# Two more Strassen-like pairs in a two-layer MLP behind attention, with their token sums made earlier and partly on another engine

## The chip, the cores and the metric

The kernel runs on one core of a Trainium2 chip. The metric is device time in microseconds (us), the median of three runs. A core has five engines with queues of their own that run in order: TensorE (PE) multiplies matrices into PSUM, VectorE (DVE) and ScalarE (ACT) compute on SBUF and PSUM, GpSimd (POOL) computes on SBUF, and SyncE (SP) issues the DMAs here. Semaphores order work between them.

## The reference, cut to what matters

```
attn = clustered attention over q, k, v            # batch 2, 8 heads, 768 tokens, 64 per head
x = attn as (1536 tokens, 512)
h = x @ w_in;  x = max(0.01 h, h) @ w_out          # layer one, d_ff 2048
h = x @ w_in2; r = max(h, 0); out = (r * r) @ w_out2   # layer two, d_ff 2048
```

All inputs are fp32 and the weights arrive as 64-bit floats that the kernel decodes itself.

## The kernel before

Each fp32 operand of a matmul is held as a rounded high part and the rest, the low part (xh and xl, wh and wl, gh and gl, th and tl), and each product is three matmuls: high by high, high by low, low by high. All of these matmuls are 128 x 128 by 512 columns.

After attention come two layers, m = 0 (layer one) and m = 1 (layer two). The 1536 tokens are three blocks b of 512 columns. The 2048 hidden rows are 16 slices f of 128, and the outer loop takes them in pairs (f, f + 1). For a pair, `g1` multiplies a block of x with a slice of w_in (12 matmuls, "a unit"), `act` turns the result into gh and gl, and `g2` multiplies these with a slice of w_out into four PSUM banks o0 to o3 (12 matmuls). After the second slice of a pair, `flush` adds the four banks to the running sum `acc` in SBUF; in a layer's first pair it copies them there on ScalarE (L860). In layer one's last pair `flush` makes the input of layer two: the sum (VectorE, L867), its high part xh (ScalarE, L868), and its low part xl (GpSimd, L869).

A pair is either plain or a quad. A plain pair runs six units. A quad (`quad`) computes blocks 0 and 1 of both slices together as a 2 by 2 problem with seven half products of 6 matmuls in place of eight (a Strassen-Winograd scheme); block 2 stays plain. It needs four differences of x, called t1 to t4 in the code: t1 = b12 - b11, t2 = b22 - t1, t3 = b22 - b12, t4 = b21 - t2, where b11 and b12 are a row chunk kk of x (0 or 1) in token blocks 0 and 1, and b21 and b22 the chunk 2 + kk. So each layer makes eight of them, once. th and tl hold t1 to t3; t4 takes the place of a part of x (`t_last`, L978 and L979). A quad also needs a third set of weights for each pair, sums of the two decoded slices (`sum_pieces`, four GpSimd operations at L197, a ScalarE cast, a GpSimd low part at L134).

PLAIN gives the number of plain pairs at the start of each layer. `step_list` gives the steps of a pair in TensorE's order; each engine gets its instructions in the order in which the steps are written out, except in layer one's first pair, which is ordered by a planner together with the end of attention. Steps of a plain pair are 12 matmuls each: units with the `g2` of earlier units between them. After step i of a pair, the table TURN issues pieces of the decoding of the next pair's weights: pieces 0 to 6 are the load (L147), a scaling on ScalarE (L156), three VectorE operations (L160, L166, L173), the high part on ScalarE (L133), and the low part on GpSimd (L134). The staging buffer `wraw` is single, so the load of a block waits for the last VectorE operation (L173) of the block before.

SUMS says after which step ("turn", counted from the start of the layer) the differences are made. In the kernel before, x is put together again from xh and xl on VectorE (`whole`, L960), the differences and low parts are made on GpSimd (L947 and L953), and the high parts on ScalarE (L950); the first of them come at turns 11 and 22 in layer one and 3 and 11 in layer two.

In layer two `act` is four instructions: relu (ScalarE, L803), square (VectorE, L806), high (ScalarE, L815) and low (VectorE, L818).

Of the kernel before, what the change touches and what calls it, by code (L numbers as in the profile page):

```python
# [8 lines left out]
F32 = mybir.dt.float32  # L9
# [4 lines left out]
ALU = mybir.AluOpType  # L14
# [39 lines left out]
def attention_moe_moe_kernel(  # L54
# [9 lines left out]
    nc = tc.nc  # L64
# [12 lines left out]
    NBLK = NT // N  # L77
    PLAIN = (3, 2)
    EARLY = 1
# [749 lines left out]
    def g2(m, b, f):  # L829
# [3 lines left out]
        for o in range(4):  # L833
# [20 lines left out]
            if last:  # L854
                flush(m, b, f // 2, o, outs[o])

    def flush(m, b, g, o, ps):
        a = acc[:, b, o]
        if g == 0:
            nc.scalar.copy(out=a, in_=ps)  # L860
            return
        if g < NF // 2 - 1:
            nc.vector.tensor_tensor(out=a, in0=ps, in1=a, op=ALU.add)  # L863
            return
        if m == 0:
            c = slice(b * N, (b + 1) * N)
            nc.vector.tensor_tensor(out=a, in0=ps, in1=a, op=ALU.add)  # L867
            nc.scalar.copy(out=xh[:, o, c], in_=a)  # L868
            nc.gpsimd.tensor_tensor(  # L869
                out=xl[:, o, c], in0=a, in1=xh[:, o, c].bitcast(F32), op=ALU.subtract  # L870
            )
        else:
            ob = tmp()
            nc.vector.tensor_tensor(out=ob, in0=ps, in1=a, op=ALU.add)
            r = b * N + o * 128
            nc.sync.dma_start(out=out[r : r + 128, :], in_=ob)
# [57 lines left out]

    def whole(k, b):
        h, l = x_in(k, b)
        t = tmp()
        nc.vector.tensor_tensor(out=t, in0=h.bitcast(F32), in1=l.bitcast(F32), op=ALU.add)
        return t

    def t_pieces(kk):

        st = {}

        def minus(out, x, y, *tag):
            st[out] = tmp(*tag)
            nc.gpsimd.tensor_tensor(out=st[out], in0=st[x], in1=st[y], op=ALU.subtract)  # L947

# [7 lines left out]

        def whole(out, k, b):
            h, l = x_in(k, b)
            st[out] = tmp()
            nc.vector.tensor_tensor(  # L960
                out=st[out], in0=h.bitcast(F32), in1=l.bitcast(F32), op=ALU.add
            )

        return [
            lambda: (whole("b12", kk, 1), whole("b11", kk, 0)),
            lambda: (minus("t1", "b12", "b11"), whole("b22", 2 + kk, 1)),
            lambda: (minus("t2", "b22", "t1"), high(0, "t1")),
            lambda: (low(0, "t1"), high(1, "t2")),
            lambda: (minus("t3", "b22", "b12"), whole("b21", 2 + kk, 0)),
            lambda: (low(1, "t2"), high(2, "t3")),  # L970
            lambda: (minus("t4", "b21", "t2", "t4", 2), t_late.update({kk: st["t4"]})),
            lambda: low(2, "t3"),
        ]

# [39 lines left out]
    )  # L1014
    SUMS = ((11, 22), (3, 11))
    LAST = (30, 19)
    order = ctx.enter_context(ExitStack())
# [10 lines left out]
    def pair_after(m, f):  # L1028
        return (m, f + 2) if f + 2 < NF else (m + 1, 0)

    prev = []
    for m in range(2):
        turn = 0
        sums = {}
        for kk in range(2):
            for i, t in enumerate(t_pieces(kk)):
                sums.setdefault(SUMS[m][kk] + i, []).append(t)
            sums.setdefault(LAST[m] + kk, []).append(lambda kk=kk: t_last(kk))
        for f in range(0, NF, 2):
# [14 lines left out]
            for i, step in enumerate(seq):  # L1054
                step()
                if (m, f, i) == (0, 0, 0):
                    for j in range(7):
                        piece((0, 0, 1), j)
                    piece((0, 2, 0), 0)
                for k, j in TURN[i] if i < len(TURN) else ():  # L1060
                    piece((*later, 0) if k == 3 else (*after, k), j)
                for t in sums.pop(turn, ()):
                    t()
                turn += 1
# [47 lines left out]
```

## Time and profile before

| what | value |
|---|---|
| median of 3 runs | 762.04 us (761.23 to 762.39) |
| the profiled execution | 762.55 us, of it span 760.8 us |
| granted TensorE clock | 1.0 of full speed |
| instructions in the span | 11079 |

The time of an execution is that of the whole program; the span is from the first instruction to the last one that the profiler saw. All times below are us from the start of the span. A matmul of 512 columns is shown as 0.39 us busy, but the next one starts 0.23 us after it; the ends overlap.

### The profile page before, as it was taken

What the parts mean: (1) busy time and instruction counts of PE and PEld (TensorE: products, weight loads), DVE (VectorE), ACT (ScalarE), POOL (GpSimd) and SP (SyncE); (2) the same over time, 40 slices, a digit from 0 to 9 for tenths busy, and PEclk for the clock granted to TensorE, in tenths of its full rate; (3) what the DMA queues carried; (4) which work ended last, traced back from release to release, by engine and by line L of the source; (5) the groups of instructions that cost most, each with busy time, mean ns of one, the idle gap of its engine ahead of it and who ended that gap; (6) DMA issues with size and microseconds to landing.
All of it is one profiled execution on the core that took longest, in us unless ns stands there. A gap on an engine that the chain in (4) does not pass through costs nothing.

```text
span 760.8 us, 11079 instructions
## 1 busy us (share of the span) xinstructions
PE 746.1 (98%) x4060; PEld 650.0 (85%) x4060; DVE 569.7 (75%) x861; ACT 440.4 (58%) x812; POOL 383.4 (50%) x344
## 2 busy tenths in 40 slices
PE   8999999999999999999999999999999999999998
PEld 8899999999989888888888888887878888888886
DVE  5999999999999545876666576656678787686755
ACT  6988988988998564344444343546544345443430
POOL 2889889889855326561442314356461441423400
PEclk9999999999999999999999999999999999999999
DMA  7494563572601212111121112203111211122004
GB/s 230 96 219 110 123 167 107 123 170 69 154 23 61 107 56 111 55 56 56 59 108 56 55 56 84 83 1 111 56 56 61 94 68 55 56 77 90 1 1 165
DMA packets 16902, 66.35 MB, mean 87 GB/s; under 512 B 3152, under 2 KB 4048, under 8 KB 11856
## 3 DMA queue, kind: packets, MB, share of 16 engines
q1 hardware_dynamic: 16848, 65.65, 29.1%
q8 instruction: 32, 0.52, 0.3%
q14 instruction: 22, 0.18, 0.1%
HBM read 44.60 MB, written 3.15 MB: 63 GB/s over the span
## 4 chain that ended last, share of the span: by engine, by line
PE 78%; DVE 13%; ACT 5%; issue 1%; DMA 1%; POOL 1%; DVEq 0%; SPq 0%; ACTq 0%; POOLq 0%
PE o L847 32%; PE h L770 29%; PE A L487 6%; PE S L389 5%; PE T L452 5%; DVE el L469 4%; DVE nm L412 3%; ACT e L422 2%; DMA wraw<-w 1%; PE warm L242 1%; DVE xt L509 1%; DVE ds L319 1%; ACT acc L860 1%; DVE m L318 1%; DVE h L806 1%
## 5 line engine op out<-in xcount | busy, mean ns | idle before, releaser
L134 POOL TENSOR_TENSOR wl<-wt,wh 128x1024 fp32r<-128x1024 f32 x32 | 77.0, 2407 | 132.8 <-ACT wh L133 132.8
L818 DVE TENSOR_TENSOR gl<-h,gh 128x512 fp32r<-128x512 f32 x96 | 65.8, 690 | 70.8 <-ACT h L813 50.2
L770 PE MATMUL h<-xl,wh 128*128 128x512 f32 x296 | 115.4, 390 | 0.0
L770 PE MATMUL h<-xh,wl 128*128 128x512 f32 x296 | 115.0, 389 | 0.0
L770 PE MATMUL h<-xh,wh 128*128 128x512 f32 x296 | 114.8, 390 | 0.0
L863 DVE TENSOR_TENSOR acc<-o,acc 128x512 f32<-128x512 f32 x144 | 92.6, 685 | 12.1 <-PE o L847 12.1
L469 DVE TENSOR_TENSOR el<-T,eh 128x512 fp32r<-128x512 f32 x144 | 94.4, 683 | 4.3 <-ACT eh L463 3.2
L439 POOL TENSOR_SCALAR e<-e,r 128x768 f32<-128x768 f32 x96 | 87.7, 925 | 19.4 <-DVE r L436 13.2
L412 DVE TENSOR_REDUCE nm<-S 128x1 f32<-128x768 f32 x96 | 90.9, 948 | 4.2 <-PE S L297 2.4
L422 ACT ACTIVATE e<-S,nm 128x768 f32<-128x768 f32 x96 | 87.3, 909 | 11.0 <-DVE nm L412 6.8
L389 PE MATMUL S<-hb 128*128 128x384 f32 (+1 forms) x384 | 90.2, 349 | 1.9 <-ACT e L422 1.2
L463 ACT CAST eh<-T 128x512 fp32r<-128x512 f32 x144 | 79.8, 589 | 13.4 <-PE T L452 13.1
L487 PE MATMUL A<-eh,vv 128*128 128x256 f32 x288 | 79.6, 306 | 2.0 <-DVE xt L509 2.0
L452 PE MATMUL T<-ident,e 128*128 128x128 f32 x576 | 79.6, 273 | 1.0 <-DVE el L469 1.0
L847 PE MATMUL o<-wh,gh 128*128 128x512 f32 x192 | 75.0, 391 | 2.8 <-DVE acc L863 1.7
L847 PE MATMUL o<-gl,wh 128*128 128x512 f32 x192 | 74.8, 390 | 0.0
L847 PE MATMUL o<-wh,gl 128*128 128x512 f32 x192 | 74.7, 389 | 0.0
L847 PE MATMUL o<-gh,wl 128*128 128x512 f32 x192 | 74.7, 389 | 0.0
L847 PE MATMUL o<-wl,gh 128*128 128x512 f32 x192 | 74.7, 389 | 0.0
L847 PE MATMUL o<-gh,wh 128*128 128x512 f32 x192 | 73.6, 389 | 0.0
L487 PE MATMUL A<-el,vv 128*128 128x256 f32 x288 | 72.5, 282 | 0.4 <-DVE el L469 0.4
L452 PEld LDWEIGHTS T<-ident,e 128*128 128x128 f32 x576 | 69.0, 144 | 4.0 <-POOL e L439 1.3
(130 smaller groups left out, 1537.1 us busy)
## 6 DMA issues: line engine op xcount, KB each, us to landing
wraw<-w SPq DMA_DIRECT2D x32, 1024.0 KB, 4.7
hb<-spl SPq DMA_DIRECT2D x14, 576.0 KB, 4.7
hb<-spl SPq DMA_DIRECT2D x42, 192.0 KB, 5.1
rqk<-qk SPq DMA_DIRECT2D x16, 384.0 KB, 3.8
rv<-v SPq DMA_DIRECT2D x8, 384.0 KB, 3.6
out<-q SPq DMA_DIRECT2D x12, 256.0 KB, 2.0
twice<-qk SPq DMA_DIRECT2D x8, 192.0 KB, 6.3
hb<-st SPq DMA_DIRECT2D x56, 24.0 KB, 2.0
```

The source lines that it names most:

```text
L134: return lambda: nc.gpsimd.tensor_tensor(out=wl, in0=t, in1=wh.bitcast(F32), op=ALU.subtract)
L389: nc.tensor.matmul(out=s[:, c, 0:HALF], lhsT=hb[0:k, a, i * 128 : (i + 1) * 128], rhs=hb[0:k, b, c * HALF : (c + 1) * HALF], start=(a == 0 ...
L412: nc.vector.tensor_reduce(out=n, in_=s_t[t][:, :, 0:HALF], axis=AX.XY, op=ALU.max, negate=True)
L422: nc.scalar.activation(out=e.rearrange("p (a b) -> p a b", a=2), in_=s_t.pop(t)[:, :, 0:HALF], func=AF.Exp, bias=n_t.pop(t), scale=1.0, ac ...
L439: nc.gpsimd.tensor_scalar(out=e_t[t], in0=e_t[t], scalar1=r_t[t // 2][:, t % 2 : t % 2 + 1], scalar2=1.0, op0=ALU.mult, op1=ALU.mult,)
L452: nc.tensor.transpose(T[:, o : o + 128], e_t[2 * u + b][:, kc * 128 : (kc + 1) * 128], ident)
L463: nc.scalar.copy(out=eh[:, 2 * g : 2 * g + 2, :].rearrange("p a b -> p (a b)"), in_=T_t[u, g])
L469: nc.vector.tensor_tensor(out=el[:, 2 * g : 2 * g + 2, :].rearrange("p a b -> p (a b)"), in0=T_t.pop((u, g)), in1=eh[:, 2 * g : 2 * g + 2, ...
L487: nc.tensor.matmul(out=A, lhsT=w, rhs=m[:, kc, :], start=(kc == 0 and i == 0), stop=(kc == KC - 1 and i == 1),)
L770: nc.tensor.matmul(out=out, lhsT=l, rhs=r, start=(first and i == 0), stop=(i == n - 1), skip_group_check=not first,)
L847: nc.tensor.matmul(out=outs[o], lhsT=l, rhs=r, start=(first and i == 0), stop=(last and i == 2),)
L863: nc.vector.tensor_tensor(out=a, in0=ps, in1=a, op=ALU.add)
```

## The change

Layer one has two plain pairs where it had three, and layer two one where it had two, so that one more pair in each layer is a quad. The differences of x are therefore made earlier: in layer one from turn 3 on, and in layer two from the last three steps of layer one (turns -3 to -1) to turn 3, with t4 put in place at turns 7 and 8. t1, t2 and t4 move from GpSimd to VectorE, t3 stays on GpSimd. Layer two takes x for them from `acc`, where layer one's fp32 outputs of blocks 0 and 1 stand, and no longer adds xh and xl up. For block 2, layer one's last sum is left in its PSUM bank, and its four low parts are made on VectorE, from PSUM, after the fourth sum; before, GpSimd made them from `acc`. In layer two's first pair the decode pieces 1 to 3 of the second weight block come a step later (TURN_SEAM).

```diff
--- before.py
+++ after.py
@@ -75,7 +75,7 @@
     HALF = S // 2
     N = 512
     NBLK = NT // N
-    PLAIN = (3, 2)
+    PLAIN = (2, 1)
     EARLY = 1
     RING = 6
     SIDE = 4
@@ -854,6 +854,8 @@
             if last:
                 flush(m, b, f // 2, o, outs[o])
 
+    x_low = []
+
     def flush(m, b, g, o, ps):
         a = acc[:, b, o]
         if g == 0:
@@ -864,11 +866,21 @@
             return
         if m == 0:
             c = slice(b * N, (b + 1) * N)
-            nc.vector.tensor_tensor(out=a, in0=ps, in1=a, op=ALU.add)
-            nc.scalar.copy(out=xh[:, o, c], in_=a)
-            nc.gpsimd.tensor_tensor(
-                out=xl[:, o, c], in0=a, in1=xh[:, o, c].bitcast(F32), op=ALU.subtract
-            )
+            x, eng = (ps, nc.vector) if b == 2 else (a, nc.gpsimd)
+            nc.vector.tensor_tensor(out=x, in0=ps, in1=a, op=ALU.add)
+            nc.scalar.copy(out=xh[:, o, c], in_=x)
+            if b == 2:
+                x_low.append((o, c, x))
+                if o < 3:
+                    return
+                todo = list(x_low)
+                x_low.clear()
+            else:
+                todo = [(o, c, x)]
+            for o, c, x in todo:
+                eng.tensor_tensor(
+                    out=xl[:, o, c], in0=x, in1=xh[:, o, c].bitcast(F32), op=ALU.subtract
+                )
         else:
             ob = tmp()
             nc.vector.tensor_tensor(out=ob, in0=ps, in1=a, op=ALU.add)
@@ -932,45 +944,61 @@
 
         return first, second, third
 
-    def whole(k, b):
-        h, l = x_in(k, b)
-        t = tmp()
-        nc.vector.tensor_tensor(out=t, in0=h.bitcast(F32), in1=l.bitcast(F32), op=ALU.add)
-        return t
-
-    def t_pieces(kk):
+    def t_ops(m, kk):
 
         st = {}
 
-        def minus(out, x, y, *tag):
-            st[out] = tmp(*tag)
-            nc.gpsimd.tensor_tensor(out=st[out], in0=st[x], in1=st[y], op=ALU.subtract)
-
-        def high(i, t):
-            nc.scalar.copy(out=th[:, i, kk], in_=st[t])
-
-        def low(i, t):
-            nc.gpsimd.tensor_tensor(
-                out=tl[:, i, kk], in0=st[t], in1=th[:, i, kk].bitcast(F32), op=ALU.subtract
-            )
-
         def whole(out, k, b):
+            if m:
+                st[out] = acc[:, b, k]
+                return
             h, l = x_in(k, b)
             st[out] = tmp()
             nc.vector.tensor_tensor(
                 out=st[out], in0=h.bitcast(F32), in1=l.bitcast(F32), op=ALU.add
             )
 
-        return [
-            lambda: (whole("b12", kk, 1), whole("b11", kk, 0)),
-            lambda: (minus("t1", "b12", "b11"), whole("b22", 2 + kk, 1)),
-            lambda: (minus("t2", "b22", "t1"), high(0, "t1")),
-            lambda: (low(0, "t1"), high(1, "t2")),
-            lambda: (minus("t3", "b22", "b12"), whole("b21", 2 + kk, 0)),
-            lambda: (low(1, "t2"), high(2, "t3")),
-            lambda: (minus("t4", "b21", "t2", "t4", 2), t_late.update({kk: st["t4"]})),
-            lambda: low(2, "t3"),
-        ]
+        def minus(eng, out, x, y, *tag):
+            st[out] = tmp(*tag)
+            eng.tensor_tensor(out=st[out], in0=st[x], in1=st[y], op=ALU.subtract)
+
+        def high(i, t):
+            nc.scalar.copy(out=th[:, i, kk], in_=st[t])
+
+        def low(i, t):
+            nc.gpsimd.tensor_tensor(
+                out=tl[:, i, kk], in0=st[t], in1=th[:, i, kk].bitcast(F32), op=ALU.subtract
+            )
+
+        def t4():
+            minus(nc.vector, "t4", "b21", "t2", "t4", 2)
+            t_late[kk] = st["t4"]
+
+        def t1():
+            if m:
+                whole("b12", kk, 1)
+                whole("b11", kk, 0)
+                whole("b22", 2 + kk, 1)
+                whole("b21", 2 + kk, 0)
+            minus(nc.vector, "t1", "b12", "b11")
+
+        return {
+            "w12": lambda: whole("b12", kk, 1),
+            "w11": lambda: whole("b11", kk, 0),
+            "w22": lambda: whole("b22", 2 + kk, 1),
+            "w21": lambda: whole("b21", 2 + kk, 0),
+            "t1": t1,
+            "t2": lambda: minus(nc.vector, "t2", "b22", "t1"),
+            "t3": lambda: minus(nc.gpsimd, "t3", "b22", "b12"),
+            "t4": t4,
+            "h1": lambda: high(0, "t1"),
+            "h2": lambda: high(1, "t2"),
+            "h3": lambda: high(2, "t3"),
+            "l1": lambda: low(0, "t1"),
+            "l2": lambda: low(1, "t2"),
+            "l3": lambda: low(2, "t3"),
+            "h4": lambda: t_last(kk),
+        }
 
     def t_last(kk):
         h, l = x_in(kk, 1)
@@ -1012,8 +1040,23 @@
         ((0, 1),), ((0, 2), (0, 3)), ((0, 4), (1, 0)), ((0, 5),), ((0, 6), (1, 1)),
         ((1, 2), (1, 3)), ((1, 4), (2, 0)), ((1, 5), (1, 6), (3, 0)), ((2, 1),), ((2, 2),),
     )
-    SUMS = ((11, 22), (3, 11))
-    LAST = (30, 19)
+    TURN_SEAM = (
+        ((0, 1),), ((0, 2), (0, 3)), ((0, 4), (1, 0)), ((0, 5),), ((0, 6),), ((1, 1), (1, 2)),
+        ((1, 3), (1, 4), (2, 0)), ((1, 5), (1, 6), (3, 0)), ((2, 1),), ((2, 2),),
+    )
+    SUMS = (
+        {
+            3: "w12.0 w11.0", 4: "t1.0 w22.0", 5: "h1.0 t3.0", 6: "l1.0 t2.0", 7: "h2.0 w21.0",
+            8: "l2.0 t4.0 h3.0", 9: "l3.0", 10: "w12.1 w11.1", 11: "t1.1 w22.1", 12: "h1.1 t3.1",
+            13: "l1.1 t2.1", 14: "h2.1 w21.1", 15: "l2.1 t4.1", 16: "h3.1", 17: "l3.1",
+            20: "h4.0", 21: "h4.1",
+        },
+        {
+            -3: "t1.0 t1.1", -2: "t2.0 t2.1 h1.0 h1.1", -1: "t3.0 t3.1 h2.0 h2.1",
+            0: "t4.0 l1.0 l1.1", 1: "t4.1 l2.0 l2.1 h3.0", 2: "l3.0 h3.1", 3: "l3.1",
+            7: "h4.0", 8: "h4.1",
+        },
+    )
     order = ctx.enter_context(ExitStack())
     pieces = {}
 
@@ -1028,14 +1071,16 @@
     def pair_after(m, f):
         return (m, f + 2) if f + 2 < NF else (m + 1, 0)
 
+    t_by = [[t_ops(m, kk) for kk in range(2)] for m in range(2)]
+
+    def sums(m, turn):
+        for op in SUMS[m].get(turn, "").split():
+            name, kk = op.split(".")
+            t_by[m][int(kk)][name]()
+
     prev = []
     for m in range(2):
         turn = 0
-        sums = {}
-        for kk in range(2):
-            for i, t in enumerate(t_pieces(kk)):
-                sums.setdefault(SUMS[m][kk] + i, []).append(t)
-            sums.setdefault(LAST[m] + kk, []).append(lambda kk=kk: t_last(kk))
         for f in range(0, NF, 2):
             if (m, f) == (0, 2):
                 order.enter_context(
@@ -1057,10 +1102,12 @@
                     for j in range(7):
                         piece((0, 0, 1), j)
                     piece((0, 2, 0), 0)
-                for k, j in TURN[i] if i < len(TURN) else ():
+                table = TURN_SEAM if (m, f) == (1, 0) else TURN
+                for k, j in table[i] if i < len(table) else ():
                     piece((*later, 0) if k == 3 else (*after, k), j)
-                for t in sums.pop(turn, ()):
-                    t()
+                sums(m, turn)
+                if m == 0 and f == NF - 2:
+                    sums(1, i - len(seq))
                 turn += 1
```

## Rows read from the trace of the kernel before

**Rows 1.** The page, busy time of each engine, share of the span and instructions.

```profile
PE 746.1 (98%) x4060; PEld 650.0 (85%) x4060; DVE 569.7 (75%) x861; ACT 440.4 (58%) x812; POOL 383.4 (50%) x344
```

**Rows 2.** Windows: plain pair, quad, layer two's first pair; busy (count) PE, PEld, DVE, ACT, POOL.

```profile
273.00:305.70 32.70, 32.70 (x146) 27.06 (x145) 17.32 (x22) 15.31 (x25) 14.06 (x9) 1.00 0.17 65
...
338.30:369.60 31.30, 31.30 (x140) 25.92 (x139) 21.02 (x29) 13.38 (x20) 10.63 (x8) 1.00 0.19 68
500.10:528.30 28.20, 27.56 (x122) 22.47 (x122) 18.70 (x23) 15.18 (x25) 13.37 (x10) 1.00 0.16 54
```

**Rows 3.** Timeline of TensorE in layer two: start, us, instruction, idle before and its releaser.

```profile
518.95 0.39 PE L770 MATMUL h<-xh,wl 128*128 128x512 f32 x1
519.98 0.50 PE L847 MATMUL o<-wh,gh 128*128 128x512 f32 x1 [0.64 <-ACT acc L860]
520.32 0.39 PE L847 MATMUL o<-wl,gh 128*128 128x512 f32 x1
...
531.63 0.50 PE L847 MATMUL o<-wh,gh 128*128 128x512 f32 x1 [0.47 <-ACT acc L860]
...
555.38 0.47 PE L847 MATMUL o<-wh,gh 128*128 128x512 f32 x1 [1.69 <-DVE acc L863]
```

**Rows 4.** Timeline of ScalarE in layer two's first two pairs.

```profile
514.54 0.60 ACT L803 ACTIVATE t<-h 128x512 f32<-128x512 f32 x1
...
518.32 1.14 ACT L156 ACTIVATE wt<-wraw 128x1024 f32<-128x1024 f32 x1 [1.82 <-DMA wraw<-w]
519.36 2.04 ACT L860 COPY acc<-o 128x512 f32<-128x512 f32 x4
...
530.48 0.62 ACT L950 CAST th<-q 128x512 fp32r<-128x512 f32 x1 [1.93 <-POOL q L947]
```

**Rows 5.** Timeline of VectorE from the end of layer one.

```profile
498.30 2.73 DVE L867 TENSOR_TENSOR acc<-o,acc 128x512 f32<-128x512 f32 x4 [2.71 <-PE o L847]
503.69 0.70 DVE L806 SCALAR_TENSOR_TENSOR h<-h,t 128x512 f32<-128x512 f32 x1 [2.66 <-ACT t L803]
...
508.52 0.69 DVE L160 TENSOR_SCALAR wt<-wt 128x1024 int32<-128x1024 int32 x1
509.24 1.23 DVE L166 SCALAR_TENSOR_TENSOR wt<-wraw,wt 128x1024 int32<-128x1024 int32 x1
510.38 0.69 DVE L806 SCALAR_TENSOR_TENSOR h<-h,t 128x512 f32<-128x512 f32 x1
...
512.34 1.22 DVE L173 SCALAR_TENSOR_TENSOR wt<-wraw,wt 128x1024 int32<-128x1024 int32 x1
513.47 1.29 DVE L960 TENSOR_TENSOR q<-xh,xl 128x512 f32<-128x512 f32 x2
...
517.13 1.77 DVE L960 TENSOR_TENSOR q<-xh,xl 128x512 f32<-128x512 f32 x1
```

**Rows 6.** Groups by line, TensorE: shapes and count, busy us and mean ns, idle before.

```profile
L770 PE MATMUL h<-xl,wh 128*128 128x512 f32 x296 | 115.4, 390 | 0.0
...
L770 PE MATMUL h<-th,wh 128*128 128x512 f32 x66 | 25.7, 389 | 0.0
```

**Rows 7.** Groups by line from 285 us on, VectorE and GpSimd.

```profile
L818 DVE TENSOR_TENSOR gl<-h,gh 128x512 fp32r<-128x512 f32 x88 | 60.3, 691 | 60.7 <-ACT h L813 40.2 <-ACT gh L815 19.6
...
L960 DVE TENSOR_TENSOR q<-xh,xl 128x512 f32<-128x512 f32 x13 | 10.8, 853 | 0.0
...
L134 POOL TENSOR_TENSOR wl<-ws,wh 128x1024 fp32r<-128x1024 f32 x11 | 27.4, 2492 | 0.0
...
L197 POOL TENSOR_TENSOR ws<-wt 128x256 f32<-128x256 f32 x22 | 16.4, 744 | 107.7 <-DVE wt L173 107.7
...
L869 POOL TENSOR_TENSOR xl<-acc,xh 128x512 fp32r<-128x512 f32 x12 | 15.1, 1296 | 12.2 <-ACT xh L868 12.2
```

**Rows 8.** Timeline of GpSimd over the same stretch.

```profile
495.68 10.05 POOL L869 TENSOR_TENSOR xl<-acc,xh 128x512 fp32r<-128x512 f32 x8
...
517.08 1.28 POOL L947 TENSOR_TENSOR q<-q 128x512 f32<-128x512 f32 x1
```

More of the change, by code (lines that the diff above doesn't have):

```diff
@@ L933, in quad, with whole @@
         return first, second, third
-    def whole(k, b):
-        h, l = x_in(k, b)
-        t = tmp()
-        nc.vector.tensor_tensor(out=t, in0=h.bitcast(F32), in1=l.bitcast(F32), op=ALU.add)
-        return t
-    def t_pieces(kk):
-        st = {}
-        def minus(out, x, y, *tag):
+    def t_ops(m, kk):
+        st = {}
+        def whole(out, k, b):
+            if m:
+                st[out] = acc[:, b, k]
+                return
+            h, l = x_in(k, b)
+            st[out] = tmp()
+            nc.vector.tensor_tensor(
+                out=st[out], in0=h.bitcast(F32), in1=l.bitcast(F32), op=ALU.add
+            )
+        def minus(eng, out, x, y, *tag):
             st[out] = tmp(*tag)
-            nc.gpsimd.tensor_tensor(out=st[out], in0=st[x], in1=st[y], op=ALU.subtract)
+            eng.tensor_tensor(out=st[out], in0=st[x], in1=st[y], op=ALU.subtract)
         def high(i, t):
@@ L955, in low @@
             )
[L957 to L961, printed above, removed]
-            )
-        return [
-            lambda: (whole("b12", kk, 1), whole("b11", kk, 0)),
-            lambda: (minus("t1", "b12", "b11"), whole("b22", 2 + kk, 1)),
-            lambda: (minus("t2", "b22", "t1"), high(0, "t1")),
-            lambda: (low(0, "t1"), high(1, "t2")),
-            lambda: (minus("t3", "b22", "b12"), whole("b21", 2 + kk, 0)),
-            lambda: (low(1, "t2"), high(2, "t3")),
-            lambda: (minus("t4", "b21", "t2", "t4", 2), t_late.update({kk: st["t4"]})),
-            lambda: low(2, "t3"),
-        ]
+        def t4():
[25 more added lines that the diff above has]
+        }
     def t_last(kk):
```

## The prediction, made before the changed kernel was run

> **What bounds the kernel now.** The page's first part comes first: TensorE is busy for 98% of the span [rows 1]. So a change counts by the TensorE work that it removes and by the gaps that it opens or closes; other engines cost nothing while TensorE's next operand is ready. The windows then show the stages: a plain pair takes 32.70 us, a quad 31.30, both with TensorE busy throughout; layer two's first pair has gaps, 27.56 of 28.20 [rows 2]. A quad is 42 + 24 + 72 = 138 matmuls (seven half products, two units of block 2, six `g2`), so one matmul is 31.30 / 138 = 0.227 us and a step of twelve 2.72.
>
> The timeline of TensorE shows three gaps, all at layer two's beginning [rows 3]. A matmul that should start 0.23 after the one before starts 1.03 after it (518.95 to 519.98): 0.80 lost, which is the idle time shown plus 0.16 of overlapping end. So the three gaps cost 0.80, 0.63 and 1.85. The matmul behind the first follows after 0.34, not 0.23; 0.1 for each gap brings the sum to 3.6.
>
> Each gap is a `g2` that waits for its PSUM bank to be emptied by the `g2` before. In the first, ScalarE's copies (519.36) stand behind the scaling of a weight block, which waits for its DMA. That load starts when VectorE has finished the block before: L173 ends at 513.56, the scaling starts at 518.32, 4.76 later [rows 4, 5]. In the second, the copies stand behind a high part that waits 1.93 for a GpSimd difference [rows 4]. In the third VectorE itself is late.
>
> **The change, part by part.** *Two more quads.* A quad has 42 matmuls for blocks 0 and 1 where a plain pair has 48. Twelve go: 12 x 0.227 = **-2.72** (the difference of the windows, 2 x 1.40, says 2.8). The x groups should go from 296 to 280 each, the th groups from 66 to 78 [rows 6].
>
> *Two more sets of weight sums.* On GpSimd 4 x 0.74 + 2.49 = 5.5 each [rows 7], and about 1 us on ScalarE. GpSimd is busy 14.1 of 32.7 and ScalarE 15.3 of 32.7 in a plain pair [rows 2]: hidden, 0.
>
> *Layer one's earlier differences.* Six move to VectorE. One VectorE operation of this form costs 0.61 in a series (two in 1.29 at 513.47) and 1.77 where a GpSimd operation is under way (517.13) [rows 5]: 3.7 to 10.6 in all. VectorE has 15 us idle in the second pair [rows 2]. They are due at the third step of the first quad, near 311, and are issued up to turn 15, near 289. I take 0; without that cover it is the slow rival below.
>
> *The port between VectorE and GpSimd* prices the rest. L947 runs on GpSimd from 517.08 to 518.36; L960 starts at 517.13 and ends at 518.90, 0.54 after it, instead of taking 0.68 [rows 5, 8]. So an operation with both inputs in SBUF waits for the GpSimd operation in flight. Low parts from PSUM don't: L818 has a mean of 691 ns over 88, L960 853 over 13 [rows 7]. The Trainium skill says so too ("SBUF — State Buffer", section "SBUF: two separate sides"): a VectorE operation with two SBUF inputs and a GpSimd operation that reads SBUF exclude each other, each for its whole length. That rule speaks against this change. Taken literally, a waiting difference would cost 0.68 behind GpSimd's end and not 0.54, for three turns some 0.4 more: 762.6 instead of my 762.2. The row decides.
>
> *The seam of the layers.* I lay the queues out with these durations, on the clock of before, where layer two starts seven steps of 2.72 ahead of 519.18, at 500.14. In before, GpSimd makes eight low parts in a row from 495.68, one each 1.25 [rows 8].
>
> 1. VectorE finishes block 1's sums near 495.6, then has t1 and t2 for both kk. The first gets through by 496.3. Each of the other three takes turns with a low part: 1.2 + 0.54 = 1.74. t2 ends at 501.5.
> 2. Behind them stand block 2's four sums, in before 498.30 to 501.03. Now they run from 501.5 at 0.60 each and end at 503.9. The four low parts from PSUM follow (0.6 each, price by L818), to 506.3. GpSimd is rid of 5 us, which nothing waits for.
> 3. The first square of layer two starts at 506.2, not 503.69, 2.5 late. Its low part ends at 508.3; `g2` wants it at 508.75. No gap yet.
> 4. t4 of kk 0 adds 0.4 more. L160 would start at 511.4 (before 508.52) and meets a GpSimd low part of t2 that starts under 0.1 us ahead of it: 1.1. The second t4 adds 0.6: the square of unit (1,0) is 4.6 late (510.38 to 514.95). L173 meets a further low part of t3: 1.1. It ends at **519.2** instead of 513.56.
> 5. ScalarE waits for it with a weight's high part (1.0), then relu, and after VectorE's square the high part: the copies that empty the banks start at 522.04, not 519.36, though TURN_SEAM now puts them ahead of the scaling. `g2` wants o0 at 519.18 and gets it at 522.6: **3.5**.
> 6. The next load also starts at 519.2; scaling 4.76 later at 524.0. Then 1.14 + 0.6 + 0.75 + 0.6 + 0.6 + 1.23 + 1.25 (scaling, L160, a square, its high and low part, L166, L173): the block is decoded at 530.2. ScalarE's high part (1.0) and the copy of t4 (0.5) stand ahead of the relu of unit (2,1): 531.7. Relu 0.6, 0.6 for t4's low part, square 0.7, high 0.6, low 0.7, handovers 0.1: its bank is free at 534.95. The quad's second product needs that bank, at 522.66 + 3 x 2.72 + 1.36 = 532.2: **2.8**.
>
> After that the quad's slack is that of the later quads, which show no gap. The sums that were the second gap's cause are gone, and the third gap's pair is now a quad.
>
> **The sum.** -2.72 - 3.6 (the old gaps) + 3.5 + 2.8 + 0.2 (two restarts) = +0.2. The profiled execution took 762.55 (span 760.8 and 1.75 around it), which gives 762.75; against the median of 762.04, 0.51 lower, it gives **762.2**.
>
> Bounds. If no VectorE operation met GpSimd at the seam, steps 1, 4 and 6 lose 3 x 1.14, 0.4, 2 x 1.1 and 0.6; with the slack that turns up, about 0.7 of gap is left: -2.72 - 3.6 + 0.8 = -5.5, 756.5. If every difference waited for a whole 2.4 us low part of weights, the three turns would be 2.9 instead of 1.74: +3.5, 765.7. I take the alternation, since the row is of the same form and size.
>
> **The rivals.**
> *Faster: the collisions fall out otherwise.* The meetings in step 4 are decided by under 0.1 us. If VectorE goes first in both, sign and load come 2.2 earlier: 760.0. If instead t1 and t2 get through in 0.6 each, block 2's sums end at 501.0 as before, 2.9 earlier: 759.3. For it: the closeness, and that L960's mean of 853 says that most such operations ran free [rows 7]. Against it: GpSimd has a closed row of work just there [rows 8].
> *Slower: layer one's differences stall its first pair.* There the planner orders ScalarE. If a high part of t1 to t3 stands ahead of the copies that empty the banks (L860), it is the second gap of before again: 0.63 at best, 1.93 if all of the wait shows [rows 3, 4]. Three high parts of kk 0 fall there: 1.9 to 5.8, so 764.1 to 768. It decides from 1.4 on. Against it: these copies come once in the pair's first ten turns for each block, and VectorE is half idle.
> *That it doesn't do what it says* is out: the counts follow from the code.
>
> **Chances.** A run of this kernel can tell 0.2%, 1.5 us. Forecast, within 760.5 and 763.6: 0.55. Faster rival, with the part of it below 760.5: 0.29. Slower rival, and a seam chain some 1.4 us longer than laid out: 0.16. The range for 8 in 10 goes from 758.0, between the fast rival and the bound, to 764.6, the lower end of the slow one.
>
> **What would show it.** Right: 2226 matmuls of the two layers; one gap of about 3.5 at a `g2` seven steps into layer two, released by the ScalarE copies, and one of 2.8 in the quad, released by L818; t1 and t2 of layer two in VectorE at about 1.8 each; L173 ending some 19 us after layer two's start. Wrong: no long gap there (the queues overlap), gaps in layer one, or a quad in which TensorE waits for the weight sums' low part, which my layout meets with only 0.7 to spare.

## The result, and the profile after

The changed kernel takes 773.17 us in the median (770.81 to 773.62), beside 762.21 for the kernel before on the same chip: a ratio of 1.0141, 95% interval [1.0129, 1.0153]. It is 11.0 us slower; 762.2 was forecast, with a range up to 764.6. Its profiled execution has a span of 771.4 us, 10.6 more than before.

The page after, busy time by engine, against [rows 1]:

```profile
PE 746.8 (97%) x4048; PEld 650.4 (84%) x4048; DVE 584.4 (76%) x875; ACT 445.8 (58%) x820; POOL 377.7 (49%) x338
```

TensorE has its twelve instructions fewer, and still it is not less busy: some of them ran longer. The groups by line show the counts of the forecast, 280 in each x group and 78 in the first th group [rows 6]:

```profile
L770 PE MATMUL h<-xh,wh 128*128 128x512 f32 x280 | 109.4, 392 | 2.6 <-DVE gl L818 2.6
...
L770 PE MATMUL h<-th,wh 128*128 128x512 f32 x78 | 30.3, 389 | 0.0
```

The timeline of TensorE (start, us, instruction, idle before and releaser) has three gaps, against [rows 3]. Two were forecast: 3.22 idle at a `g2` of layer two, released by the copies, and 2.64 in its quad, released by L818. The longest, 6.99, is in layer one and was not.

```profile
266.86 0.39 PE L770 MATMUL h<-xh,wl 128*128 128x512 f32 x1
274.23 2.08 PE L847 MATMUL o<-gh,wh 128*128 128x512 f32 x4 [6.99 <-ACT gh L812]
276.10 0.63 PE L847 MATMUL o<-gl,wh 128*128 128x512 f32 x1
...
526.86 0.39 PE L770 MATMUL h<-xh,wl 128*128 128x512 f32 x1
530.47 0.50 PE L847 MATMUL o<-wh,gh 128*128 128x512 f32 x1 [3.22 <-ACT acc L862]
...
539.90 0.39 PE L770 MATMUL h<-xh,wl 128*128 128x512 f32 x1
542.93 0.80 PE L770 MATMUL h<-xh,wh 128*128 128x512 f32 x1 [2.64 <-DVE gl L818]
543.52 0.63 PE L770 MATMUL h<-xl,wh 128*128 128x512 f32 x1
```

Counted from start to start less 0.227, the gaps are 7.15, 3.38 and 2.80. Behind the first and the third the matmuls come 0.427 apart instead of 0.227 (276.10 to 276.53; 543.52 to 543.95), 12 and 6 of them with the first at 0.59. The windows (length, busy time and count by engine, then the granted TensorE clock) show why: behind these two gaps the clock was granted at 0.50, the lower level of 1.2 GHz, and behind the middle one at 1.00.

```profile
274.30:279.30 5.00, 5.00 (x12) 3.98 (x13) 2.77 (x4) 3.37 (x7) 1.83 (x1) 0.50 0.46 185
530.50:533.50 3.00, 3.00 (x13) 2.50 (x14) 0.64 (x2) 2.90 (x5) 0.00 (x1) 1.00 0.21 87
543.00:545.50 2.50, 2.50 (x6) 2.02 (x7) 0.69 (x1) 2.50 (x7) 2.50 (x2) 0.50 0.00 0
```

The excess over 0.227 behind the first gap adds up to 2.6, behind the third to 1.4. So the two layers lose 7.15 + 2.6 in layer one's first pair, 3.5 at the first gap of the seam with its restart, and 2.80 + 1.4 at the second: 17.4, where the kernel before loses 3.6. The difference of 13.8, less 2.72 for the matmuls that went, is 11.1, and the spans differ by 10.6.

**What happens in layer one's first pair.** The chain of work that ended last, followed back from TensorE's start at 274.23 (start, us, what), is VectorE without a break:

```profile
256.57 1.20 DVE q L957 x2
...
258.26 2.31 DVE q L963
260.57 1.24 DVE q L957
...
261.84 2.23 DVE q L963
264.06 1.70 DVE q L957
...
267.39 1.75 DVE t L963
269.14 2.21 DVE wt L166
...
271.38 1.24 DVE wt L173
```

(q L957 are the four whole sums w12, w11, w22 and w21 of the code, q L963 t1 and t2, t L963 t4.) The two whole sums at the top ran free, 0.60 each; what follows takes 1.2 to 2.3 each. Here is GpSimd in the same stretch:

```profile
257.13 2.89 POOL L134 TENSOR_TENSOR wl<-wt,wh 128x1024 fp32r<-128x1024 f32 x1 [7.97 <-ACT wh L133]
260.00 1.27 POOL L205 TENSOR_SCALAR xh<-xt 128x768 fp32r<-128x768 f32 x1
261.35 2.16 POOL L517 TENSOR_TENSOR xl<-xt,xh 128x768 fp32r<-128x768 f32 x1
263.48 1.74 POOL L963 TENSOR_TENSOR q<-q 128x512 f32<-128x512 f32 x1
265.18 5.09 POOL L969 TENSOR_TENSOR tl<-q,th 128x512 fp32r<-128x512 f32 x3
```

L205 and L517 make the high and the low part of the last attention output. GpSimd's operations follow each other from 257.13 to 270.27, and VectorE's fall in between: t1 ends 0.55 behind L134 (260.57), w22 0.54 behind L205, t2 0.56 behind L517, w21 0.55 behind t3; then L160, t4 and L166 behind one low part each. The chain from 258.26 to 272.62 is 14.4 us; the same operations without waits are 6 x 0.60 + 1.15 + 1.24 = 6.0. About 8.3 us is waiting for GpSimd.

At the end of VectorE's row stands the decoding of a weight block, and ScalarE's high part of that block (L133) stands in ScalarE's queue ahead of the relu's high part `gh`, which `g2` wants. ScalarE's timeline:

```profile
272.63 1.04 ACT L133 CAST wh<-wt 128x1024 fp32r<-128x1024 f32 x1 [6.28 <-DVE wt L173]
273.59 0.59 ACT L812 ACTIVATE gh<-h 128x512 fp32r<-128x512 f32 x1
```

ScalarE waited 6.28 for L173. The kernel before has the same order, but there L173 ends at 265.51. A window of the kernel before:

```profile
253.50:267.00 13.50, 13.50 (x67) 11.41 (x66) 6.97 (x9) 7.13 (x12) 5.40 (x4) 1.00 0.25 85
```

And VectorE's timeline in it:

```profile
262.06 0.93 DVE L160 TENSOR_SCALAR wt<-wt 128x1024 int32<-128x1024 int32 x1 [3.92 <-ACT wt L156]
...
264.28 1.23 DVE L173 SCALAR_TENSOR_TENSOR wt<-wraw,wt 128x1024 int32<-128x1024 int32 x1
```

VectorE was busy 6.97 of 13.5 us there, with 0.97 and 3.92 idle before L160 and nothing idle between L160 and L173. The change puts seven operations of kk 0 (4.2 us) and 8.3 of waiting into those 4.9 us of cover: 7.6 too much, and the gap is 7.15.

### The profile page after: what moved, and what is told of

It is laid out like the page before. It is cut to its first block, busy times and chain, and to the rows that moved or that the text cites. A ratio compares the mean times of both kernels' runs of the same rounds, so it can differ in the third digit from the quotient of the medians.

```text
span 771.4 us, 11077 instructions
## 1 busy us (share of the span) xinstructions
PE 746.8 (97%) x4048; PEld 650.4 (84%) x4048; DVE 584.4 (76%) x875; ACT 445.8 (58%) x820; POOL 377.7 (49%) x338
## 4 chain that ended last, share of the span: by engine, by line
PE 73%; DVE 19%; ACT 5%; issue 2%; DMA 1%; POOL 0%; DVEq 0%; ACTq 0%; SPq 0%; POOLq 0%
PE o L847 31%; PE h L770 27%; PE S L389 5%; PE A L487 4%; DVE el L469 4%; PE T L452 4%; DVE nm L412 4%; ACT e L422 2%; DVE q L963 1%; DVE wt L166 1%; DVE wt L173 1%; DVE xt L509 1%; ACT eh L463 1%; PE warm L242 1%; DVE ds L319 1%
## 5 line engine op out<-in xcount | busy, mean ns | idle before, releaser
L134 POOL TENSOR_TENSOR wl<-wt,wh 128x1024 fp32r<-128x1024 f32 x32 | 77.4, 2420 | 140.0 <-ACT wh L133 140.0
L818 DVE TENSOR_TENSOR gl<-h,gh 128x512 fp32r<-128x512 f32 x96 | 65.6, 690 | 70.4 <-ACT h L813 51.9
L770 PE MATMUL h<-xh,wh 128*128 128x512 f32 x280 | 109.4, 392 | 2.6 <-DVE gl L818 2.6
L770 PE MATMUL h<-xl,wh 128*128 128x512 f32 x280 | 109.6, 391 | 0.0
L770 PE MATMUL h<-xh,wl 128*128 128x512 f32 x280 | 109.3, 391 | 0.0
L865 DVE TENSOR_TENSOR acc<-o,acc 128x512 f32<-128x512 f32 x144 | 93.5, 685 | 14.3 <-PE o L847 14.3
L439 POOL TENSOR_SCALAR e<-e,r 128x768 f32<-128x768 f32 x96 | 87.7, 925 | 19.4 <-DVE r L436 13.2
L463 ACT CAST eh<-T 128x512 fp32r<-128x512 f32 x144 | 79.8, 589 | 13.4 <-PE T L452 13.1
L197 POOL TENSOR_TENSOR ws<-wt 128x256 f32<-128x256 f32 x26 | 19.3, 743 | 130.7 <-DVE wt L173 130.7
```

The costliest lines, as they stand in the source:

```text
L134: return lambda: nc.gpsimd.tensor_tensor(out=wl, in0=t, in1=wh.bitcast(F32), op=ALU.subtract)
L439: nc.gpsimd.tensor_scalar(out=e_t[t], in0=e_t[t], scalar1=r_t[t // 2][:, t % 2 : t % 2 + 1], scalar2=1.0, op0=ALU.mult, op1=ALU.mult,)
L463: nc.scalar.copy(out=eh[:, 2 * g : 2 * g + 2, :].rearrange("p a b -> p (a b)"), in_=T_t[u, g])
L770: nc.tensor.matmul(out=out, lhsT=l, rhs=r, start=(first and i == 0), stop=(i == n - 1), skip_group_check=not first,)
```

## The experiments

**Which half of the change costs what.** e1 keeps layer one as before; e2 keeps layer two.

In both the differences of the other layer are on GpSimd at the turns of before (layer two's in e2 from xh and xl again, with the table TURN and block 2's low parts on GpSimd). The diffs here and below are cut.

```diff
# e1
-    PLAIN = (2, 1)
+    PLAIN = (3, 1)
+        eng = nc.vector if m else nc.gpsimd
-            minus(nc.vector, "t1", "b12", "b11")
+            minus(eng, "t1", "b12", "b11")
-            3: "w12.0 w11.0", 4: "t1.0 w22.0", 5: "h1.0 t3.0", ...
+            11: "w12.0 w11.0", 12: "t1.0 w22.0", 13: "t2.0 h1.0", ...
# e2
-    PLAIN = (2, 1)
+    PLAIN = (2, 2)
+        eng = nc.gpsimd if m else nc.vector
-            -3: "t1.0 t1.1", -2: "t2.0 t2.1 h1.0 h1.1", ...
+            3: "w12.0 w11.0", 4: "t1.0 w22.0", 5: "t2.0 h1.0", ...
```

> Layer two's half of the change alone: three plain pairs and all differences of layer one on GpSimd at the old turns, layer two as in the changed kernel. Theory (two separate causes, one in each layer): the gaps of the changed kernel at the seam stay, 3.38 + 0.11 and 2.80 + 1.55 of matmuls at half rate, in place of 3.6; one quad less in layer one. 762.2 - 1.36 + 7.8 - 3.6 = 765.1. Rival (the seam's gaps come from layer one's new plan, which reaches the seam late): the gaps shrink, 761 or less.

> Layer one's half alone: two plain pairs in layer one with its differences as in the changed kernel; layer two, its differences and block 2's low parts as before. Theory: the 7.15 us gap in layer one's first pair and the 2.6 us of matmuls at half rate behind it stay, the three old gaps too: 762.2 - 1.36 + 9.75 = 770.6. Rival (that gap comes from the planner's other view of the whole program): under 764.

Measured: e1 763.98, ratio 1.0026 [1.0016, 1.0037]; e2 769.74, ratio 1.0100 [1.0085, 1.0115]. Layer two's half costs 2.0 us, layer one's 7.7; together 9.7 of the 11.0. e2 has the long gap alone (7.09, and 12 matmuls at half rate behind it) and the three old gaps. e1 has the seam gaps: 3.38, but here with a slow clock behind it:

```profile
523.50:526.00 2.50, 2.50 (x7) 1.91 (x7) 0.97 (x2) 1.91 (x3) 0.00 (x0) 0.50 0.00 0
```

Its second gap is then 1.27, not 2.80: what releases it is the decoding chain on ScalarE and VectorE, which does not wait for TensorE, so the time that TensorE loses earlier comes off the later gap. The two traces bear that out: the second gap ends 13.1 behind the start of the copies in one, 13.2 in the other. So the seam loses 6.5 in e1 and 7.7 in the changed kernel, which is the rest of the 11.0.

**Layer one's differences later.** e3 is the changed kernel with layer one's sums from turn 10 on instead of 3.

```diff
-            3: "w12.0 w11.0", 4: "t1.0 w22.0", 5: "h1.0 t3.0", 6: "l1.0 t2.0", 7: "h2.0 w21.0",
+            10: "w12.0 w11.0", 11: "t1.0 w22.0", 12: "h1.0 t3.0", 13: "l1.0 t2.0", ...
```

> The changed kernel with layer one's differences issued from turn 10 on (7 turns later for kk 0, 4 for kk 1, t4 put in place at 21 and 22), so that none is in the first pair, which the planner orders. Theory (VectorE's queue in the first pair, filled by differences that take turns with GpSimd, holds up the weight decoding and so ScalarE): the 7.15 gap goes and with it the matmuls at half rate; new gaps of 0 to 2 in the second pair and the first quad, since the differences are now crowded there: 763.5 to 765.5. Rival (the first pair stalls for the third set of weights or the earlier quad itself): 770 or more.

Measured: 764.54, ratio 1.0035 [1.0026, 1.0045], 8.6 less than the changed kernel. A window over the old place has TensorE busy throughout:

```profile
254.00:274.00 20.00, 20.00 (x95) 16.49 (x94) 8.61 (x11) 12.41 (x22) 7.46 (x4) 1.00 0.30 106
```

Only 0.28 (296.6) and 1.09 (318.8, in the first quad) appear instead. So the long gap comes from where the operations stand, not from the quad that they serve.

**GpSimd or VectorE's own work?** e5 was to take GpSimd's four operations of kk 0 out of the first pair; e9 does it in another way. In e5 t3, l1, l2 and l3 are written at turns 10 to 12. In e9 ScalarE's high parts are also written behind the pair, and t3 behind the first low part, so that GpSimd has no operand sooner; kk 1's operations come up to three turns later there. VectorE's seven operations stay where they are in both.

```diff
# e5
-            5: "h1.0 t3.0", 6: "l1.0 t2.0", 8: "l2.0 t4.0 h3.0", 9: "l3.0",
+            5: "h1.0", 6: "t2.0", 8: "t4.0", 10: "t3.0 l1.0 ...", 11: "h3.0 l2.0 ...", 12: "l3.0 ...",
# e9
+            6: "t2.0", 8: "t4.0", 12: "h1.0 l1.0 t3.0", 13: "h2.0 l2.0 ...", 14: "h3.0 l3.0 ...",
```

> The changed kernel with GpSimd's four operations on the differences of kk 0 (t3 and the three low parts) moved from turns 5 to 9 to turns 10 to 12; VectorE's seven operations stay in the first pair. Theory (they wait for GpSimd one by one): without 1.1 us of waiting for each of w21, L160, t4 and L166, L173 ends at 268.5 and not at 272.6, and the 7.15 us gap shrinks to about 3; with the matmuls at half rate unchanged 769, without them 766.5. Rival (VectorE's seven further operations by themselves fill the time): the gap stays near 7 and the time near 773.

> The changed kernel, but in layer one's first pair ScalarE's high parts of kk 0 are issued after the pair, so that GpSimd's low parts and its t3, which stands behind the first of them in GpSimd's queue, cannot start before; VectorE keeps all seven of its kk 0 operations at their old turns. Port theory: t1, the second whole sum and t2 still wait for the weight's and x's low parts on GpSimd, until 264.07; then nothing of GpSimd is under way, and the third whole sum, L160, t4, L166 and L173 take 0.68, 0.60, 0.68, 0.60 and 1.23: L173 ends near 268 instead of 272.6, and the gap falls from 7.15 to about 2.6. Time 766 to 769, by whether the clock still falls behind the shorter gap. Rival (the seven operations' own length and the order of VectorE's queue cause the stall, not GpSimd): the gap stays above 5.5 and the time at 771 or more.

e5 measured 770.87, ratio 1.0115 [1.0098, 1.0132], with a gap of 5.93: a miss. Its timeline of GpSimd shows t3 at 263.44 and two low parts from 265.13 all the same:

```profile
265.13 3.40 POOL L969 TENSOR_TENSOR tl<-q,th 128x512 fp32r<-128x512 f32 x2
```

Nothing was ahead of them in GpSimd's queue, and their inputs were ready, so writing them later did not make them later. Only l3 left the stretch; L166 took 1.21 instead of 2.28, and the gap lost 1.2, one wait. That agrees with the port and does not prove it.

e9 measured 768.72, ratio 1.0093 [1.0070, 1.0117]. The gap, from the matmul at 265.80, is 2.84 where 2.6 was expected. Its end in TensorE's timeline:

```profile
268.87 1.21 PE L847 MATMUL o<-gh,wh 128*128 128x512 f32 x4 [2.68 <-ACT gh L812]
```

VectorE's timeline in e9, behind GpSimd's last operation:

```profile
262.96 0.68 DVE L957 TENSOR_TENSOR q<-xh,xl 128x512 f32<-128x512 f32 x1
263.57 0.68 DVE L160 TENSOR_SCALAR wt<-wt 128x1024 int32<-128x1024 int32 x1
264.17 0.68 DVE L963 TENSOR_TENSOR t<-q 128x512 f32<-128x512 f32 x1
264.77 1.21 DVE L166 SCALAR_TENSOR_TENSOR wt<-wraw,wt 128x1024 int32<-128x1024 int32 x1
266.02 1.23 DVE L173 SCALAR_TENSOR_TENSOR wt<-wraw,wt 128x1024 int32<-128x1024 int32 x1
```

The same five operations took 1.78, 1.78, 1.75, 2.28 and 1.23 in the changed kernel. They are the same on the same engine in the same order; GpSimd is still, and ScalarE's three casts of kk 0, 0.6 each, are gone from the stretch as well. e6 below moves GpSimd's low parts and no cast, and there too the operations that had waited run free. So the waits are GpSimd's doing, and 4.3 of the 7.15 come from its four kk 0 operations. The other 2.8 is VectorE's own seven and their waits behind L134, L205 and L517, which were there before. No matmul behind e9's gap ran at half rate. A new gap of 1.79 behind 299.0 is released by VectorE (acc, L865), behind L173, L160 and L166 at 2.34, 1.78 and 2.19 beside GpSimd's moved operations; that these are its cause was not tried.

**Is the slow clock a cost of its own?** e4 puts twelve matmuls, whose result nothing reads, into the third gap, the one in layer two's quad.

```diff
             nc.scalar.copy(out=p1, in_=U)
+            for _ in range(12 if (m, f) == (1, 2) else 0):
+                nc.tensor.matmul(
+                    out=X, lhsT=w_in(f0, 0)[0], rhs=x_in(0, 0)[0], start=True, stop=True
+                )
```

> The changed kernel with 12 further matmuls (2.72 us, into a bank that is overwritten later) put into layer two's first quad ahead of its second product, where TensorE waits 2.80. Theory (TensorE's clock falls to half behind a gap of 3 us and the matmuls at 427 ns are that): no matmul at half rate there, 1.5 us less: 771.7. Rival (the slow matmuls have another cause): 773.2 and the matmuls behind the gap still at 427 ns.

Measured: 771.5, ratio 1.0125 [1.0110, 1.0140], 1.7 less than the changed kernel with twelve matmuls more. The clock behind the filled gap, where the changed kernel has 0.50 from 543.00 on:

```profile
542.27:545.00 2.73, 2.73 (x12) 2.27 (x13) 0.73 (x1) 2.73 (x7) 2.73 (x2) 1.00 0.03 6
```

The gap itself is not shorter, since the fill stands in it. What went is the 1.4 of slow matmuls. That this and the 1.7 agree is within what four runs tell.

**The parts of the seam.** (The first gap here is the one at the `g2`, the second the one in the quad.) Three edits of e1: e6 moves layer two's low parts to turns 3 to 5; e10 gives block 2's low parts back to GpSimd; e11 keeps the old table TURN in layer two's first pair. TURN_SEAM moves two pieces of the second block a step later, the scaling (piece 1) and L166 (piece 3); L160 (piece 2) has the same step in both.

```diff
# e6
-            0: "t4.0 l1.0 l1.1", 1: "t4.1 l2.0 l2.1 h3.0", 2: "l3.0 h3.1", 3: "l3.1",
+            0: "t4.0", 1: "t4.1 h3.0", 2: "h3.1", 3: "l1.0 l1.1", 4: "l2.0 l2.1", 5: "l3.0 l3.1",
# e10
-            x, eng = (ps, nc.vector) if b == 2 else (a, nc.gpsimd)
+            x, eng = (a, nc.gpsimd)
# e11
-                table = TURN_SEAM if (m, f) == (1, 0) else TURN
+                table = TURN
```

> The kernel with layer two's half alone (764.0 us), with GpSimd's six low parts of layer two's differences moved from turns 0 to 3 to turns 3 to 5. Theory (L160, L173 and a t4 each wait for a low part): the first gap falls from 3.4 to about 1, and since VectorE's and ScalarE's chain up to the quad's second product is shorter by 2, the second gap is near 3 and the sum of what is lost falls from 6.6 by 1 to 2.3: 762 to 763. Rival (VectorE is late by the mere number of its operations): the first gap stays at 3.4, the time at 764.

> The kernel of e1 (layer two alone), but block 2's low parts stay on GpSimd and read the fp32 sum in SBUF. Port theory: VectorE gives up four operations of 0.6, but GpSimd gets four of 1.25 or more in just the stretch in which VectorE's t4, L160 and L166 want the port, so the first gap does not shrink by the 2.4 that VectorE saves: 3.4 to 5, and the time 764 to 766. Rival (only the length of VectorE's queue counts): the first gap falls to about 1.0 and the time to 761.5 to 763.

> The kernel of e1 (layer two alone), but layer two's first pair keeps the old table of turns for its weight pieces, so that ScalarE's scaling of the next block stands ahead of the copies that empty the banks again. By the layout of the prediction the copies then also wait for the scaling, which starts some 4.8 after L173's end: the first gap grows from 3.4 to about 6.6, the second shrinks to about 0.5; time 766 to 768. Rival (the order on ScalarE does not matter because L173 sets the end either way): first gap 3.4 as in e1, time 764.

e6: 764.30, ratio 1.0022 [1.0010, 1.0035]. The first gap fell to 0.83 as expected, so 2.5 of its 3.38 are VectorE's waits for the moved low parts; t4, L160, L166 and L173 took 0.68, 0.68, 1.22 and 1.22 in e6. But the time did not fall. The second gap, near 3 expected, grew to 3.91, since the moved low parts met the next block's L160 (1.82), so that the chain up to the quad's second product ends only 1.5 sooner than in e1, counted from the start of the first gap, while TensorE comes 4.1 sooner (2.5 of gap, 1.6 of slow matmuls that e1 has behind it). And behind the second gap 2.7 more went to matmuls at half rate, which the expectation left out. This is the profiled execution, of 765.73; of the ten, the five with the mean granted clock at 0.998 took 762.85 to 764.08, the other five, at 0.996 or less, 764.51 to 767.39. TensorE in e6:

```profile
534.16 0.79 PE L770 MATMUL h<-xh,wh 128*128 128x512 f32 x1 [3.75 <-DVE gl L818]
```

e10: 764.42, ratio 1.0032 [1.0019, 1.0045], as expected; the first gap is 4.22. The 2.4 us that VectorE saves are gone at once: its first square of layer two then waits 2.22 for ScalarE. And GpSimd's low parts reach further into what follows: t4, L160, L166, the second t4 and L173 took 1.61, 1.08, 2.20, 1.78 and 1.62, in e1 1.33, 1.80, 1.22, 0.69 and 2.32, in all 0.9 less. The end of the gap in TensorE's timeline:

```profile
522.38 0.80 PE L847 MATMUL o<-wh,gh 128*128 128x512 f32 x1 [4.06 <-ACT acc L862]
```

So moving block 2's low parts to VectorE shortens the first gap by 0.8; the medians of e1 and e10 (763.98, 764.42) are too close to say that it shortens the time.

e11: 765.34, ratio 1.0048 [1.0033, 1.0062]. ScalarE in e11:

```profile
523.60 1.12 ACT L156 ACTIVATE wt<-wraw 128x1024 f32<-128x1024 f32 x1 [1.97 <-DMA wraw<-w]
524.61 2.04 ACT L862 COPY acc<-o 128x512 f32<-128x512 f32 x4
```

The copies stand behind the scaling and its load again, and the first gap is 6.41 (6.6 expected) against 3.38. The second is gone altogether, so the time is 0.7 under the expected 766. TURN_SEAM shortens the first gap by 3.0, and 1.4 of it shows in the time.

**A version without the long gaps.** e7 is layer two alone with t2 and one t3 on GpSimd, the other t3 on VectorE, the low parts spread to turns 1 to 9, and the weight pieces at other steps. e8 adds layer one's quad, with its differences from turn 10 on and nearly all on VectorE.

```diff
# layer two in e7 and e8 (SUMS[1] and the table)
+    {-3: "t1.0 t1.1", -2: "t2.0 h1.0 h1.1", -1: "t2.1", 0: "t3.1 h2.1", 1: "t3.0 t4.0 t4.1 l1.0",
+     2: "h2.0 l1.1", 5: "h3.1 l2.0 l2.1", 6: "h3.0", 7: "h4.1", 8: "l3.1 h4.0", 9: "l3.0"}
+    TURN_SEAM = (
+        ((0, 1), (0, 2)), ((0, 3), (0, 4), (0, 5)), (), ((0, 6), (1, 0)), ((1, 1),),
+        ((1, 2), (1, 3), (1, 4), (2, 0)), (), (), ((1, 5), (2, 1), (2, 2), (3, 0)), ((1, 6),),
+    )
# layer one in e8
+    {10: "w12.0 w11.0 w22.0 t1.0 t3.0 h1.0 l1.0", 12: "w21.0", 13: "w11.1 t2.0", ..., 23: "l1.1 l2.1 h4.0"}
```

> Layer two's half alone, spaced anew: both t2 and one t3 on GpSimd, the low parts spread over turns 1 to 9, t4 put in place at 7 and 8, and the second weight block's load a step earlier with its scaling at step 4, its three VectorE operations at 5, its high part at 8. Theory (the seam's gaps are queue order and waits at the port, not too much work): no gap over 0.5 is left and the old three are gone as well: 762.0 - 1.36 - 3.6 = 757.1. Rival (the engines have no room for the quad that early): 760 or more.

> The whole change, two and one plain pairs, with layer two spaced as in the run before and layer one's differences spread over turns 10 to 24, all but one t4 on VectorE. Theory: the full saving of 2.72 and the three old gaps: 762.0 - 2.72 - 3.6 = 755.7, with up to 1 for small gaps in layer one's second pair. Rival (a first quad this early stalls anyway): 758 or more.

Measured: e7 756.93, ratio 0.9933 [0.9918, 0.9948]; e8 756.17, ratio 0.9920 [0.9906, 0.9935]. Both beat both kernels. Windows of e8, layer one's first pair, the beginning of its first quad, and the seam:

```profile
240.50:273.00 32.50, 32.50 (x171) 27.55 (x170) 19.00 (x24) 19.63 (x34) 12.09 (x7) 1.00 0.28 98
...
311.60:312.60 1.00, 0.67 (x3) 0.28 (x2) 0.69 (x1) 1.00 (x2) 0.66 (x1) 1.00 0.00 0
500.00:528.00 28.00, 28.00 (x125) 23.20 (x124) 19.72 (x27) 17.10 (x29) 16.32 (x14) 1.00 0.22 76
```

TensorE is busy throughout in the first and the last, and waits 0.49 for one low part in the quad. e7's gain over before is the old gaps and one quad, 3.6 + 1.36 = 5.0; the ratio gives 5.1 (its interval 4.0 to 6.3), the medians of the same session 5.6. e8's 0.76 over e7 is the other 1.36 less 0.6 for that gap and its restart; their intervals overlap, so that step is worked out and not shown by the times.

## Why the prediction was wrong

**The step that failed** is "Layer one's earlier differences", at "I take 0". Its price for the six differences, 3.7 to 10.6 in all, held: in the changed kernel they take 2.31, 2.23 and 1.75 for kk 0 and 0.68, 1.78 and 0.68 for kk 1, 9.4 in all. (Two are above its 1.77 apiece, which came from a meeting with a GpSimd operation of 1.28; they stand behind the longer L134 and L517.) Left out were the four whole sums of kk 0, which moved along, so that its seven operations took 10.4 us, and the 2.1 that L160 and L166 waited among them. But the cover decides. The 15 idle us were read in the second pair [rows 2], where the differences used to be made, and the due time (311) was compared with the time of issue (289). Yet kk 0's operations stand at turns 3 to 9, in the first pair, where VectorE had 4.9 us idle ahead of a weight block that ScalarE, and behind it TensorE, wait for in order. A difference that is due much later still delays everything behind it on its own engine. Measured: 7.15 of gap, and 2.6 of slow matmuls behind it; e3 takes both away, e9 shows that 4.3 of the gap are GpSimd's four kk 0 operations.

**The term that was missing** is TensorE's clock. A gap was priced at its length and a restart at 0.1. Behind the second seam gap 1.4 more went to matmuls at the granted clock of 0.50, as 2.6 did behind the long one. The Trainium skill ("TensorE: Matmul & The Clock Gate", section "Part 1: The HAM clock gate") says that the slow rate is the default and that activity releases the full one; the rows here show the two rates, 0.427 and 0.227 from start to start, and no run shows which is the default. Together 7.15 + 2.6 + 1.4 is 11.2, near the 11.0 between forecast and result.

**The seam was right, step by step, and in step 6 partly by luck.** Layer two starts 7.9 later than on the clock of before, by the place of the first gap (526.86 against 518.95). With 7.9 added, the forecast times stand beside VectorE after, against [rows 5]:

```profile
505.81 3.48 DVE L963 TENSOR_TENSOR q<-acc,q 128x512 f32<-128x512 f32 x2
509.21 2.48 DVE L870 TENSOR_TENSOR o<-o,acc 128x512 f32<-128x512 f32 x4
511.60 2.47 DVE L881 TENSOR_TENSOR xl<-o,xh 128x512 fp32r<-128x512 f32 x4
513.99 0.68 DVE L806 SCALAR_TENSOR_TENSOR h<-h,t 128x512 f32<-128x512 f32 x1
...
519.15 1.80 DVE L160 TENSOR_SCALAR wt<-wt 128x1024 int32<-128x1024 int32 x1
...
524.67 2.33 DVE L173 SCALAR_TENSOR_TENSOR wt<-wraw,wt 128x1024 int32<-128x1024 int32 x1
```

Step 1, t2 ends at 509.4: 509.29. Step 2, block 2's sums and low parts end at 511.8 and 514.2: 511.69 and 514.07. Step 3, the first square at 514.1: 513.99. Step 4, L160 meets a low part at 519.3 and L173 another, ending at 527.1: 519.15 with 1.80, and 527.00. For steps 5 and 6, ScalarE after, against [rows 4]:

```profile
529.83 2.06 ACT L862 COPY acc<-o 128x512 f32<-128x512 f32 x4
531.74 1.16 ACT L156 ACTIVATE wt<-wraw 128x1024 f32<-128x1024 f32 x1
...
538.08 1.05 ACT L133 CAST wh<-wt 128x1024 fp32r<-128x1024 f32 x1 [3.15 <-DVE wt L173]
```

The copies were laid out for 529.9, the scaling for 531.9, the block's end for 538.1. The gaps came to 3.38 and 2.80 where 3.5 and 2.8 were forecast.

Within step 6 two things are otherwise. The scaling has no wait for its load in the row; it starts as the copies end, 0.1 from when the load was due. And the forecast put t4's low part (L1007) behind the relu, at 0.6. In the run it stands beside the relu (539.55 to 540.15) and takes 1.18, in VectorE's timeline:

```profile
539.74 1.18 DVE L1007 TENSOR_TENSOR xl<-t,xh 128x512 fp32r<-128x512 f32 x1 [1.69 <-POOL ws L197]
```

It meets one of GpSimd's weight sums there:

```profile
539.65 0.73 POOL L197 TENSOR_TENSOR ws<-wt 128x256 f32<-128x256 f32 x1
```

It ends 0.54 behind that, at 540.92; the forecast has 540.8 and an operation of 0.60 would have ended at 540.34. The two errors cancel.

**The port's price held.** A waiting operation ended 0.54 to 0.56 behind GpSimd's, as in the row it was taken from [rows 5, 8], and not 0.68, the other reading that the prediction priced. The Trainium skill ("SBUF — State Buffer", section "SBUF: two separate sides") says that whichever of the two starts first keeps the pair of ports for its whole length; the timelines of the first pair agree, for both engines take turns there. It lists, besides operations with two SBUF inputs, those in a mode that takes both ports. L160, with one input, waits as well here (1.78 against 0.68 in e9); whether it runs in such a mode no run shows.

**The quads, the weight sums.** -2.72 is borne out by the counts, and half of it by e7's sum. The weight sums, priced at nothing, are not quite hidden: by the meeting just shown some 0.6 of the second gap is theirs, an estimate from 1.18 against 0.60, since no run takes them away. No gap of TensorE is a direct wait for them.

**The rivals.** The slower one had the place, layer one's first pair, and the idea that ScalarE's order passes a late operation on to TensorE. It named another operation (a th high part ahead of the copies; it was a weight's high part ahead of `gh`) and at most 5.8 us, since it counted no row of port waits and no clock. Of the signs of a wrong forecast, "gaps in layer one" is the one that came. The faster rival's mechanism, collisions that fall otherwise, is what e7 does on purpose: 756.9, below its 759.3 even without layer one's quad, because there both gaps go.

## What to carry to other kernels

When an operation is moved earlier, read its cover in the stretch where it will stand in its engine's queue, and not where its result is due: list what stands behind it there, and who waits for that. With VectorE and GpSimd both on SBUF operands, price each VectorE operation by the GpSimd operation that it meets and not by its own length; the same seven operations are 4.2 us alone and were 10.4 among GpSimd's. And a gap of TensorE can cost up to four fifths of its length again in matmuls at the lower clock (2.6 behind 7.15, 1.4 behind 2.80, 2.7 behind 3.91, in e3 2.8 behind 3.36), or nothing but the restart (0.1 behind 3.38 in the changed kernel).

## What the runs showed of the hardware that was not expected

- Gaps of the same length were followed by the lower clock in one kernel and not in another. The first seam gap, 3.36 to 3.38 in six kernels, had matmuls at 0.427 behind it in e1, e3 and e5, and at 0.227 in the changed kernel, e4 and e9. Near 2.8, e9's gap in layer one had none of them behind it, the gaps in the quad of the changed kernel and of e9 had some. The kernels with such gaps also vary more from run to run (e1 over 763.38 to 766.82 in ten, e9 over 766.59 to 770.16 in four, before over 761.29 to 763.27 in nineteen). The mean granted clock sorts the runs of e6, but not those of e1, whose two at 0.994 took 763.41 and 763.50, among its shortest; so the cause is open.
- An engine's queue is an order, not a time: in e5 GpSimd ran t3 and two low parts, written three to five turns later, at the same moment as in the changed kernel, since nothing stood ahead of them.
- GpSimd pays for a meeting too: in the first pair t3 takes 1.74 and a low part 1.70 where VectorE's operations alternate with them, against 1.28 and 1.30 elsewhere [rows 7, 8].
